# The MLP's second product by Strassen's scheme: seven block products for every two chunks and two token tiles

## The chip, the cores and the metric

The kernel runs on one core of one Trainium2 chip. The metric is the device time of one execution in microseconds (us); three runs of the kernel before took 801.2, 802.67 and 804.05 us, so its median is 802.67 us. The engines are named as in the profile: PE is TensorE (PEld its weight loads), DVE is VectorE, ACT is ScalarE, POOL is GpSimd, and SP is SyncE, whose queue issues most of the DMAs.

## What is computed

One transformer block on 2048 tokens of width 640. Its first half is an adaptive layer norm and a linear attention with 32 heads; its second half, which the change touches, is a second adaptive layer norm and an MLP with 1728 hidden features and a squared ReLU:

```python
h = _layernorm(x, axis=-1) * (1 + cb) + sb
x = x + gb * _B_ref(h, B_w1, B_b1, B_w2, B_b2)

def _B_ref(x, w1, b1, w2, b2):
    h = jnp.einsum("bsd,df->bsf", x, w1) + b1
    zero = jnp.zeros_like(h)
    r = jnp.where(h > zero, h, zero)
    h = r * r
    out = jnp.einsum("bsf,fd->bsd", h, w2) + b2
    return out
```

`sb`, `cb` and `gb` are vectors of 640 numbers worked out from the condition `c` and `w_mod`.

## The kernel before

All inputs are float32. Each operand of a large product is split into a high part, rounded to the type that TensorE reads in one pass (`fp32r`), and a low part, the rest; a product is then three matmuls, high by high, high by low and low by high (`three`, `mm` at line 76). ACT makes the high part with a copy, DVE the low part with a subtraction (`lo`, line 86). Every matmul of the kernel's products is put down to line 76 and every low part to line 86, so groups are told apart by their tiles.

The program has three stages: the projections with the attention's running sums; the attention's output with the product by `wo` (tile `pwo`); and the MLP. The MLP works on eight blocks (`j` = 0 to 7) of two token tiles, 256 tokens each, and on 14 chunks of hidden features (`f` = 0 to 13), 128 in each but the last, which has 64.

For each block and chunk `up(j, f)` makes the hidden values of 128 features for 256 tokens: 15 matmuls, five chunks of the width by three terms, with 256 columns moving (10 for the last chunk). They go to a bank of the pool `psB`, tile `up`. ACT applies the bias and the ReLU (line 1123), DVE squares (line 1124), ACT makes the high part (line 1125), and DVE the low part (line 86, tile `r`). Two chunks later `down(j, f)` takes the result as the stationary operand and the chunk of the second weight matrix, `W2[f]`, as the moving one: for each of the two token tiles, and for the columns 0 to 383 and 384 to 639 of the output (`CUT`), three matmuls into a bank of its own (`pj`, tiles `acc`), 12 in all (8 for the last chunk, where two terms are enough). The four banks collect over the 14 chunks. At the block's end DVE multiplies each by the gate (line 1155) and adds the residual (line 1156), and SP stores it (line 1160).

Beside that, a block makes the next block's input: loads (lines 965, 966), the sum with the attention's output (line 970) and its store (line 971), the layer norm (`ln_parts`: sums and squares on ACT, small steps on POOL at lines 318 to 325), ten transposes on PE (tile `tb`) whose results ACT scales (lines 347, 348) and DVE splits (`t_out`). During block 0, and a little before it, the two weight matrices are loaded (lines 901, 904), split on ACT (line 911) and DVE (line 86, tile `w`), and from then on they stay in SBUF.

The order of the work: in the stage ahead of the MLP the order of PE, DVE, ACT and POOL is written out by hand (`tc.manual_schedule`). In the MLP the instructions are given in the order of the loop, and a planner, which has its own costs, chooses the order on each engine. SP's order is the planner's in both. The only DMA that POOL issues stands at line 470, in the first stage.

Of the kernel before, what the change touches and what calls it, by code (L numbers as in the profile page):

```python
# [15 lines left out]
P = 128  # L16
# [21 lines left out]
W2_AT = 48  # L38
W_AT = (
# [5 lines left out]
W_LONG = {"w0", "w1", "w3", "w5", "w7", "w9", "w14", "w20", "k", "q0", "q1", "late0", "late1"}  # L45
BUFS = {"x": 2, "k": 2, "q0": 1, "q1": 1, "s1": 5, "s2": 2, "s3": 3, "s4": 5}
# [3 lines left out]
def kernel(  # L50
# [47 lines left out]
    tiny.tile([P, 16], F32, name="fill2")  # L98
    psA = ctx.enter_context(tc.tile_pool(name="psA", bufs=1, space=PS))
# [3 lines left out]
    def tok2(tag, name, at=0, pool=None):  # L103

        bufs = 1
        if tag == "w":
            tag = f"w{next(w_at)}"
        elif pool is None:
            bufs = BUFS[tag]
        t = (pool or mem).tile([P, 2 * D + (128 if tag in W_LONG else 0)], F32, tag=tag, name=name, bufs=bufs)  # L110
        return t[:, at : at + 2 * D].rearrange("p (s d) -> p s d", s=2)

    def row(tag, name):
        return mem.tile([P, D], F32, tag=tag, name=name, bufs=BUFS[tag])

# [43 lines left out]
    p12 = ExitStack()  # L159
    pc = p12.enter_context(tc.tile_pool(name="pc", bufs=1))  # L160
# [3 lines left out]
    mask5 = pc.tile([80, 40], F32, name="mask5")  # L164
    for v in vt:
        nc.gpsimd.memset(v, 0.0)
        nc.gpsimd.memset(v[:, :, 60:61], 1.0)
# [38 lines left out]
    def load_x(j):  # L206
        XB[j] = tok2("x", f"xb{j}")
# [103 lines left out]
    def ln_parts(xt, nm):  # L311
# [3 lines left out]
        for i in range(2):  # L315
            same = xt[:, i] if nm[0] == "a" else row("s3", f"same{nm}_{i}")
# [3 lines left out]
        for i in range(2):  # L320
            junk = row("s3", f"junk{nm}_{i}")
# [9 lines left out]
    def layer_norm(xt, nm):  # L331
        for _ in ln_parts(xt, nm):
# [12 lines left out]
    def t_out(cols, hT, d, nm, p):  # L345
        hf = row("s3", f"hf{nm}_{d}")[:, :256]
# [366 lines left out]
    psB = ctx.enter_context(tc.tile_pool(name="psB", bufs=3, space=PS, reuse_waits="tile"))  # L713
# [53 lines left out]
    def load_e(t):  # L767
# [4 lines left out]
        ET[t] = tok2(("k", "k", "x")[t % 3], f"el{t}")  # L772
# [112 lines left out]
    def prep_load(k, f, w):  # L885
# [6 lines left out]
        if EARLY_ROWS <= i < EARLY_ROWS + 4:  # L892
            if i % 2 == EARLY_ROWS % 2:
                RAWT.append(tok2("w", f"rawt{i}"))
# [29 lines left out]
    preps = [("1", f) for f in range(EARLY)]  # L924
    for f in range(NF):
        preps += [("2", f)] + ([("1", EARLY + f)] if EARLY + f < NF - 1 else [])
    preps += [("1", NF - 1)]
# [4 lines left out]
    def p_load(n=1):  # L932
        for _ in range(n):
            if todo["load"]:
                k, f = todo["load"].pop(0)
                prep_load(k, f, places.pop(0)(f"w{k}_{f}"))
# [19 lines left out]
    def load_x1(j):  # L956
        XM[j] = tok2("x", f"xm{j}")
        if j:
            XX[j] = [row("s2", f"xx{j}_{i}") for i in range(2)]
        else:  # L960
            both = tok2("x", "xx0")
# [6 lines left out]
    def add_x(j):  # L968
        for i in range(2):
            nc.vector.tensor_tensor(XM[j][:, i], XM[j][:, i], XX[j][i], op=ALU.add)  # L970
        nc.sync.dma_start(X1[j], XM[j])

    def layer2(j):
        add_x(j)
        layer_norm(XM[j], f"b{j}")

    def t2(j, d):
        if d == 0:
            H2[j] = ht(f"h2_{j}", j, (0, 96))
        t_unit(XM[j], cols_b, H2[j], d, f"b{j}", bank(f"tb{j}_{d}") if j == 0 or d % 2 else None)  # L980

    NB = NT // 2
    places += [new("w")] * 21 + [new(tag) for tag in ("k", "k", "q0", "q1")]
    places += [lambda nm, i=i: wslot(nm, f"late{i}", late[0]) for i in range(2)]
    places += [lambda nm: row("s1", nm)[:, None, :].bitcast(F32R)]
    assert len(places) == 2 * NF
# [30 lines left out]
    for j in range(NB):  # L1017
# [69 lines left out]
        if j == 5:  # L1087
            add_x(0)
# [11 lines left out]
        if j == 7:  # L1100
            p_hi(3)
            p_lo(4)
# [5 lines left out]
    late.append(ctx.enter_context(tc.tile_pool(name="late", bufs=1, reuse_waits="tile")))  # L1108

    def up(j, f):  # L1110
        p = bank(f"up{j}_{f}")
        terms = []
        n = FS[f]
# [5 lines left out]
        mm(p[:, :256], terms)  # L1119
        r = feat("s3", f"r{j}_{f}")  # L1120
        t = R2[j, f] = feat("s4", f"r2_{j}_{f}").bitcast(F32R)
        if n == P:
            nc.scalar.activation(r[:, 0], p[:, :256], AF.Relu, bias=b1_t[:, f : f + 1])  # L1123
# [137 lines left out]
```

## Time and profile before

| | us |
|---|---|
| median of three runs | 802.67 (801.2 to 804.05) |
| the profiled execution, its own time | 802.27 |
| its span, first to last instruction | 800.5 |
| first matmul of the MLP | 409.82 into the span |
| mean granted TensorE clock | 0.998 of full speed |

Times in the text are microseconds from the start of the span unless they are durations. A busy PE means that a matmul is somewhere in the pipe: the mean duration of one matmul in a group is about twice to two and a half times the distance between two of them, so the cost of a matmul is read from the chain of waits, where a run of 15 has its own length. Three views are used: the page's parts, the groups of instructions by line and shape, and the chain of waits that ended last, as a list in order of time.

### The profile page before, as it was taken

How to read it: one execution, taken by the hardware profiler on the slowest of the kernel's cores; microseconds unless marked ns; L12 is line 12 of the kernel's file. 1: busy time of each engine (PE TensorE's matmuls, PEld its weight loads, DVE VectorE, ACT ScalarE, POOL GpSimd, SP SyncE). 2: the span in 40 equal slices, each digit the busy share in tenths (PEclk: the TensorE clock that was granted, in tenths of full speed). 3: DMA queues.
4: the chain of work that ended last, by engine and by line, in shares of the span. 5: the costliest groups of instructions: out<-in, count | busy, mean ns of one | idle time of the engine just before them, and what ended most of it. 6: DMA issues, size and time to landing. Idle time of an engine off the chain costs nothing.

```text
span 800.5 us, 14885 instructions
## 1 busy us (share of the span) xinstructions
PE 789.8 (99%) x6085; PEld 761.6 (95%) x6085; DVE 494.8 (62%) x822; ACT 416.6 (52%) x942; POOL 75.0 (9%) x157
## 2 busy tenths in 40 slices
PE   9999999999999999999999999999999999999997
PEld 8899999999999878898899999999999999999997
DVE  4499889999788688993555753434434343353423
ACT  4667675576753355565777544354443534444321
POOL 3001021010000114331100000000000001000000
PEclk9999999999999999999999999999999999999999
DMA  8713326423120243321447330211303113030000
GB/s 325 293 35 128 114 83 203 147 85 115 67 100 1 80 168 132 116 83 67 148 142 253 117 132 2 97 68 34 133 2 130 34 67 100 1 132 1 35 1 34
DMA packets 30108, 80.13 MB, mean 100 GB/s; under 512 B 3600, under 2 KB 4112, under 8 KB 30040
## 3 DMA queue, kind: packets, MB, share of 16 engines
q1 hardware_dynamic: 27672, 73.83, 26.6%
q10 hardware_dynamic: 2304, 5.24, 1.7%
q8 instruction: 48, 0.79, 0.4%
q14 instruction: 20, 0.16, 0.1%
q0 software_dynamic: 64, 0.10, 0.0%
HBM read 55.47 MB, written 23.59 MB: 99 GB/s over the span
## 4 chain that ended last, share of the span: by engine, by line
PE 82%; DVE 8%; ACT 4%; DMA 2%; POOL 2%; issue 1%; SPq 0%; ACTq 0%; DVEq 0%; POOLq 0%
PE acc L76 23%; PE up L76 22%; PE pk L76 8%; PE pq L76 7%; PE pv L76 7%; PE pwo L76 5%; PE kvp L417 2%; DVE dn L785 2%; DVE scr L783 2%; PE te L824 2%; PE tb L337 1%; PE ta L337 1%; DMA xx<-in_x 1%; DVE ezb L804 1%; DMA raw_k<-in_wk 1%
## 5 line engine op out<-in xcount | busy, mean ns | idle before, releaser
L76 PE MATMUL acc<-w,r 128*128 128x256 f32 (+1 forms) x1312 | 216.0, 309 | 0.6 <-ACT r L1125 0.4
L76 PE MATMUL up<-h,w 128*128 128x256 f32 x1640 | 210.2, 276 | 0.0
L76 PEld LDWEIGHTS up<-h,w 128*128 128x128 f32 x1640 | 198.5, 188 | 0.1
L76 PEld LDWEIGHTS acc<-w,r 128*128 128x128 f32 x1312 | 196.9, 188 | 1.0 <-ACT r L1125 0.6
L1123 ACT ACTIVATE r<-up,b_t 128x256 f32<-128x256 f32 x104 | 48.8, 472 | 133.9 <-PE up L76 133.9
L1124 DVE TENSOR_TENSOR r<-r 128x256 f32<-128x256 f32 x104 | 43.8, 424 | 119.2 <-ACT r L1123 119.2
L76 PE MATMUL pwo<-wo,ot 128*128 128x256 f32 (+3 forms) x512 | 83.2, 315 | 0.1
L76 PE MATMUL pk<-wk,hT 128*128 128x384 f32 (+1 forms) x480 | 77.3, 312 | 0.9 <-ACT hT L348 0.9
L76 PEld LDWEIGHTS pwo<-wo,ot 128*128 128x128 f32 (+1 forms) x512 | 75.7, 188 | 1.9 <-ACT ot L861 0.4
L76 PE MATMUL pq<-wq,hT 128*128 128x384 f32 (+1 forms) x480 | 75.0, 311 | 0.4 <-ACT k L393 0.4
L76 PE MATMUL pv<-wv,hT 128*128 128x384 f32 (+1 forms) x480 | 75.2, 309 | 0.0
L76 PEld LDWEIGHTS pk<-wk,hT 128*128 128x128 f32 x480 | 71.7, 188 | 2.7 <-ACT hT L348 1.1
L1125 ACT ACTIVATE r<-r 128x256 fp32r<-128x256 f32 x104 | 42.8, 413 | 56.9 <-DVE r L1124 56.8
L76 PEld LDWEIGHTS pq<-wq,hT 128*128 128x128 f32 x480 | 70.7, 188 | 1.5 <-ACT k L393 0.9
L76 PEld LDWEIGHTS pv<-wv,hT 128*128 128x128 f32 x480 | 70.6, 188 | 0.4
L86 DVE TENSOR_TENSOR r<-r,r 128x256 fp32r<-128x256 f32 x112 | 47.2, 422 | 30.5 <-ACT r L1125 29.5
L86 DVE TENSOR_TENSOR h<-hfb,h 128x256 fp32r<-128x256 f32 x40 | 16.9, 424 | 28.9 <-ACT h L348 28.7
L445 DVE TENSOR_REDUCE rs_q<-eq 128x64 f32<-128x1280 f32 x16 | 23.5, 1472 | 14.8 <-ACT eq L404 14.8
L318 POOL TENSOR_SCALAR smb<-smb 128x2 f32<-128x2 f32 x8 | 1.8, 221 | 301.1 <-ACT sameb L317 301.1
L393 ACT ACTIVATE k<-pk 128x384 f32<-128x384 f32 (+1 forms) x32 | 13.0, 434 | 25.0 <-PE pk L76 24.9
L787 POOL TENSOR_TENSOR dn<-dn,rs_q 128x64 f32<-128x64 f32 x16 | 14.0, 873 | 128.1 <-DVE dn L785 128.1
L408 DVE TENSOR_REDUCE sk<-ek 128x64 f32<-128x1280 f32 x16 | 23.7, 1479 | 3.5 <-ACT ek L404 3.5
(185 smaller groups left out, 1039.9 us busy)
## 6 DMA issues: line engine op xcount, KB each, us to landing
esp<-eq SPq DMA_DIRECT2D x12, 640.0 KB, 3.1
el<-esp SPq DMA_DIRECT2D x12, 640.0 KB, 3.8
rw<-in_w SPq DMA_DIRECT2D x23, 320.0 KB, 3.4
wm<-in_w_mod SPq DMA_DIRECT2D x20, 320.0 KB, 3.8
xb<-in_x SPq DMA_DIRECT2D x8, 640.0 KB, 4.0
a<-at ACTq DMA_DIRECT2D x16, 320.0 KB, 2.1
xm<-a SPq DMA_DIRECT2D x16, 320.0 KB, 3.2
xx<-in_x SPq DMA_DIRECT2D x16, 320.0 KB, 3.3
```

What stands on the lines that cost most here:

```text
L76: nc.tensor.matmul(o, a, b, start=first and i == 0, stop=last and i == len(terms) - 1, skip_group_check=skip,)
L86: (eng or nc.vector).tensor_tensor(out_lo, full, hi.bitcast(F32), op=ALU.subtract)
L337: nc.tensor.transpose(p[:, i * P : (i + 1) * P], xn[:, i, d * P : (d + 1) * P], ident)
L408: nc.vector.tensor_reduce(s, heads(flat(e)), axis=AX.X, op=ALU.add)
L417: nc.tensor.matmul(kvp[64 * c : 64 * c + 64, g // 4, a : a + 2 * n].rearrange("p (s n) -> p s n", s=2), v[:, u], e[:, :, o : o + n], start ...
L445: nc.vector.tensor_reduce(s, heads(flat(e)), axis=AX.X, op=ALU.add)
L783: nc.vector.tensor_tensor(z, flat(ET[t]), flat(zb), op=ALU.mult)
L785: nc.vector.tensor_reduce(dn.rearrange("p s h -> p (s h)"), heads(z), axis=AX.X, op=ALU.add)
L824: nc.tensor.transpose(p[:m, a : a + P], EU[2 * j + i][:, b : b + m], ident)
L1123: nc.scalar.activation(r[:, 0], p[:, :256], AF.Relu, bias=b1_t[:, f : f + 1])
L1124: nc.vector.tensor_tensor(r[:, 1], r[:, 0], r[:, 0], op=ALU.mult)
L1125: nc.scalar.activation(t[:, 0], r[:, 1], AF.Copy)
```

## The change

Two chunks and two token tiles make a 2 by 2 matrix of 128 x 128 blocks, A11 and A12 for the first token tile, A21 and A22 for the second; the two chunks of the second weight matrix by the column ranges L (0 to 383) and R (384 to 639) make another, with ranges that are not equally wide. Before, the product of the two took eight block products. Now seven are formed, in the manner of Strassen: sums of the four A blocks (S1 to S4) are multiplied by weight chunks or sums of them. Four of the seven have a moving operand of 384 columns, three of 256. The seven results are collected over the pairs of chunks and combined once at the block's end.

- This form is used in blocks 2 to 7 for the pairs n = 0 to 5 (in block 7 for n = 0 to 4). The last pair, with the chunk of 64, the pair n = 5 of block 7, and the blocks 0 and 1 (`PLAIN = 2`) keep the eight products, as `down_plain`.
- The sums of the A blocks are made on DVE in every pair, from the squared values in float32; four blocks of sums are then split into high and low part (`split_s`) besides A11, A12, A22 (`split_a`).
- The sums of weights are made once, in block 1 and the start of block 2 (`t_load`, `t_sums`, `t_split`), and stored in DRAM (`TD`), three pieces for each pair: a and c of 128 x 2 x 384, b of 128 x 2 x 256 float32. One more sum takes the place of the range R of `W2[2n]` in SBUF. In blocks 2 to 7 every pair fetches its three pieces into small ring buffers with DMAs that POOL issues (`t_fetch`): two buffers for a, one for b, one for c.
- The accumulators: products 1, 2, 4 and 5 have one bank each, 3 shares a bank with the fourth plain region (`x`), 6 and 7 share one. The hidden values get one bank (`up`), its halves for even and odd chunks.
- The whole MLP's order on PE, DVE, ACT and POOL is now written by hand. Within a pair PE runs `up(j, 2n)`, the first part of the previous pair's products, `up(j, 2n+1)`, the second part. POOL takes over the sum of residual and bias (`add_bias`).
- The layer norm of the next block is cut into six pieces placed by hand (`LN_AT`...), transposes are done two units at a time, the weights of the MLP are split four at a time after every pair of block 0, and in the last step before the MLP `p_hi(3)` goes and `p_lo(4)` becomes `p_lo(3)`.

The core of the diff:

```diff
     def up(j, f):
-        p = bank(f"up{j}_{f}")
+        n, k = FS[f], f % 2
+        p = UP2[:, :256] if k and j < PLAIN else UP[:, 256 * k : 256 * k + 256]
...
+        t = FT[j, f // 2]
+        r = t[:, A12 : A22 + 1] if k else t[:, 0:8:7]
...
         if n == P:
-            nc.scalar.activation(r[:, 0], p[:, :256], AF.Relu, bias=b1_t[:, f : f + 1])
-            nc.vector.tensor_tensor(r[:, 1], r[:, 0], r[:, 0], op=ALU.mult)
-            nc.scalar.activation(t[:, 0], r[:, 1], AF.Copy)
-            lo(t[:, 1], r[:, 1], t[:, 0])
+            nc.scalar.activation(r, p, AF.Relu, bias=b1_t[:, f : f + 1])
+            nc.vector.tensor_tensor(r, r, r, op=ALU.mult)
+    def sums(j, n):
+        t = FT[j, n]
+        for o, a, b, op in ((S1, A21, A22, ALU.add), (S3, A11, A21, ALU.subtract),
+                            (S2, S1, A11, ALU.subtract), (S4, A12, S2, ALU.subtract)):
+            nc.vector.tensor_tensor(t[:, o], t[:, a], t[:, b], op=op)
+    def split_a(j, n, parts=(0, 1)):
...
+        if n < NP - 1:
+            nc.scalar.activation(a[:, 0, :3], t[:, :3], AF.Copy)
+            lo(a[:, 1, :3], t[:, :3], a[:, 0, :3])
+    def split_s(j, n):
+        t = FT[j, n]
+        a = RS[j, n] = p3.tile([P, 2, 4, P], F32, tag="rs", name=f"rs{j}_{n}").bitcast(F32R)
+        nc.scalar.activation(a[:, 0], t[:, S1 : S4 + 1], AF.Copy)
+        lo(a[:, 1], t[:, S1 : S4 + 1], a[:, 0])
+    RINGS = (("a", 384, 2), ("b", 256, 1), ("c", 384, 1))
+    def t_fetch(j, n, r):
+        RING[j, n, r] = ring(r, f"ring{j}_{n}_{r}")
+        nc.gpsimd.dma_start(RING[j, n, r], TD[n][r].bitcast(F32R))
+    def down_pair(j, n, part):
+        v, w = W2[2 * n], W2[2 * n + 1]
+        last = n == NF // 2 - 2 - (j == NB - 1)
+        if part:
+            todo = ("5", S1, RING[j, n, "a"], L), ("6", S2, v, R), ("3", S4, w, R), ("7", S3, RING[j, n, "b"], slice(0, 256))
+        else:
+            todo = ("1", A11, v, L), ("2", A12, w, L), ("4", A22, RING[j, n, "c"], L)
+        for reg, st, m, c in todo:
+            prod(j, reg, block(j, n, st), m, c, last and reg in "1567")
+    def first_combos(j):
+        y0, y1 = Y[j] = [row("s2", f"y{j}_{i}") for i in range(2)]
...
+        nc.scalar.activation(y0[:, L], p["1"], AF.Copy)
+        nc.scalar.activation(y1[:, 256:384], p["5"][:, 256:], AF.Copy)
+        add(y1[:, q], y0[:, q], p["6"])
+        add(y0[:, R], y1[:, q], p["5"][:, q])
+        add(y1[:, q], y1[:, q], p["7"])
+        add(y1[:, R], y1[:, q], p["5"][:, q])
+    def t_split(n):
+        a, b = TR_[n]
+        for r, w in (("a", a[:, L]), ("b", TR_[n, "b"][:, 1].bitcast(F32)), ("c", b[:, L]), (None, b[:, R])):
...
+            nc.scalar.activation(t[:, 0], w, AF.Copy)
+            lo(t[:, 1], w, t[:, 0])
+            if r:
+                nc.sync.dma_start(TD[n][r], t.bitcast(F32))
-    LAG = 2
-    seq = [(j, f) for j in range(NB) for f in range(NF)]
-    for n, (j, f) in enumerate(seq):
...
+    by_hand = tc.manual_schedule(engines={ET_.PE, ET_.DVE, ET_.Activation, ET_.Pool})
+    by_hand.__enter__()
+    for j in range(NB):
+        for n in range(NP):
...
+            up(j, 2 * n)
+            if prev and not plain(*prev):
+                split_s(*prev)
+            down(0)
+            if j < PLAIN:
+                layer(j + 1, 2 * n)
+            if 0 < m < NP - 2:
+                t_split(m - 1)
...
+            if twice:
+                t_fetch(j, n, "c")
+                t_fetch(j, n, "a")
...
+            up(j, 2 * n + 1)
...
+            split_a(j, n, (0, 1) if (j, n) != (NB - 1, NP - 1) else (1,))
+            if twice:
+                sums(j, n)
+            if j < PLAIN or n:
+                down(1)
+            if twice:
+                t_fetch(j, n, "b")
...
+            layer(j + 1, 2 * n + 1)
+            if 0 <= m < NP - 2:
+                t_sums(m)
...
+            prev = j, n
+    last_downs(NB - 1)
```

`down(k)` runs `down_plain` or `down_pair` for the previous pair, `twice` is true where the pair goes by the seven products, and `m` counts the pairs from the second of block 1 on. `add_bias(j)` adds the bias to the two residual tiles of a block on POOL, two additions of 128 x 640.

More of the change, by code (lines that the diff above doesn't have):

```diff
@@ L329, in ln_parts, with layer_norm @@
         yield
[L331 to L332 removed]
+    def layer_norm(xt, nm, spare=None):
+        for _ in ln_parts(xt, nm, spare):
             pass
```

389 lines of the change are left out of this document (291 added, 98 removed).

## The prediction

> **What bounds the kernel now.** I read the page first: the busy shares, and the chain that ended last.
>
> ```profile
> PE 789.8 (99%) x6085; PEld 761.6 (95%) x6085; DVE 494.8 (62%) x822; ACT 416.6 (52%) x942; POOL 75.0 (9%) x157
> ...
> PE 82%; DVE 8%; ACT 4%; DMA 2%; POOL 2%; issue 1%; SPq 0%; ACTq 0%; DVEq 0%; POOLq 0%
> ...
> L76 PE MATMUL acc<-w,r 128*128 128x256 f32 (+1 forms) x1312 | 216.0, 309 | 0.6 <-ACT r L1125 0.4
> L76 PE MATMUL up<-h,w 128*128 128x256 f32 x1640 | 210.2, 276 | 0.0
> ```
>
> PE is busy nearly always and carries 82% of the chain; its matmuls on `acc` and `up` waited 0.6 us in all. An average over stages proves little, so the busy times by block of the MLP come next (busy PE, PEld, DVE, ACT, POOL; then clock, DMA share, GB/s).
>
> ```profile
> 409.80:463.00 53.20, 52.56 (x414) 52.09 (x413) 37.01 (x71) 35.84 (x75) 1.31 (x4) 1.00 0.53 174
> ...
> 607.30:655.40 48.10, 48.10 (x382) 48.10 (x381) 19.88 (x48) 20.90 (x48) 1.59 (x4) 1.00 0.21 69
> ```
>
> In a later block PE never pauses, DVE and ACT are free more than half the time, the clock is full. There the end is set by how many columns PE streams. The chain of waits in order of time (start, length, what) gives the price of a matmul.
>
> ```profile
> 462.89 2.15 PE up L76 x19
> ...
> 607.21 2.15 PE up L76 x19
> 612.33 1.72 PE acc L76 x12
> ...
> 631.15 1.70 PE up L76 x15
> ...
> 655.31 2.15 PE up L76 x19
> ```
>
> 15 matmuls of 256 columns take 1.70 us: 0.113 each. The 12 of a chunk's `acc` are six of 384 and six of 256: 1.72 - 6 x 0.113 = 1.04, so 0.173 for one of 384. Width is what is paid for. The same mark returns after 655.31 - 607.21 = 48.10 us: one block.
>
> **The change part by part.**
>
> *What PE loses.* Two chunks cost 24 matmuls before, 12 of each width: 3.44 us. Seven products by three terms are 21: four products of 384 and three of 256, so 12 of 384 and 9 of 256, 3.10 us. Because the column ranges are unequal, the saved product is a narrow one: 3 x 0.113 = 0.34 us for a pair. Pairs: six in each of blocks 2 to 6, five in block 7, 35 in all. **Gain 35 x 0.34 = 11.9 us.** `up`, the transposes and the plain pairs keep their matmuls. Nothing else on PE's stream is late behind this gain so long as the other engines deliver; so the rest of the sum is stalls.
>
> *The steady pair, from its first `up`.* PE: `up` 0 to 1.70; products 1, 2, 4 (nine of 384, 1.56) to 3.26; second `up` to 4.96; products 5, 6, 3, 7 (1.54) to 6.50. The other engines' steps, with the hops between them, stand in the groups and in the time line of block 3's end:
>
> ```profile
> 603.88 0.47 ACT L1123 ACTIVATE r<-up,b_t 128x256 f32<-128x256 f32 x1 [3.08 <-PE up L76]
> ...
> 604.39 0.42 DVE L1124 TENSOR_TENSOR r<-r 128x256 f32<-128x256 f32 x1 [2.98 <-ACT r L1123]
> 604.85 0.42 ACT L1125 ACTIVATE r<-r 128x256 fp32r<-128x256 f32 x1 [0.49 <-DVE r L1124]
> ...
> 605.90 1.31 PE L76 MATMUL acc<-w,r 128*128 128x384 f32 x8
> 606.16 0.47 ACT L1123 ACTIVATE r<-up,b_t 128x256 f32<-128x256 f32 x1 [0.89 <-PE up L76]
> ```
> ```profile
> L86 DVE TENSOR_TENSOR r<-r,r 128x256 fp32r<-128x256 f32 x104 | 43.9, 422 | 29.8 <-ACT r L1125 29.5
> L347 ACT ACTIVATE hfb<-tb,cols_b 128x256 f32<-128x256 f32 x40 | 22.4, 560 | 0.8 <-ACT at L879 0.4 <-PE pwo L76 0.2
> L911 ACT ACTIVATE w<-rw 128x640 fp32r<-128x640 f32 x24 | 17.0, 730 | 5.8 <-DMA rw<-in_w 5.0 <-ACT at L879 0.8
> L970 DVE TENSOR_TENSOR xm<-xm,xx 128x640 f32<-128x640 f32 x16 | 13.1, 824 | 14.8 <-DMA xx<-in_x 14.8
> L1155 DVE TENSOR_TENSOR y<-acc,gb_b 128x384 f32<-128x384 f32 x16 | 8.9, 553 | 6.5 <-PE acc L76 6.5
> ```
>
> A hop from ACT to DVE or back is 0.04 us (603.88 + 0.47 to 604.39); ACT's ReLU starts 0.26 after PE has gone on to its next group (605.90 to 606.16). Between 256 columns (422 ns) and 640 (824) DVE pays 1.03 ns a column, so estimates are 0.29 us for 128, 0.55 for 384 (the row says 553), 0.69 for 512; ACT between 413 and 730 the same way: 0.52 for 384, 0.62 for 512.
>
> A blocks: the second ReLU starts at 5.22 and ends 5.69, square to 6.15, copy of three blocks to 6.7, low part to 7.3. Product 1 needs it at 6.50 + 1.70 = 8.20: **0.9 us in hand**. Sums: four times 0.29, to 8.45, which is 1.95 of the next pair; `split_s` copies after the first ReLU (2.43) to 3.05, low part to 3.8; product 5 needs it at 4.96: 1.2 in hand. DVE's work in a pair is 0.42 + 0.69 + 0.42 + 0.55 + 1.17 = 3.25 of 6.50 us, and a block's other DVE work (low parts of the transposes 5 x 0.42, sum with x 2 x 0.82, combining and four ends 3.6, gate and residual 4 x 0.82) adds 10.6 over seven pairs. DVE goes from 19.9 us to about 32 of 46 in a block, ACT from 20.9 to about 24. Both fit, and a misplaced piece of 0.8 us is what the margin takes. I take nothing for the steady pair here; if the cover went, a slip of 0.1 in every pair would be 3.5 us.
>
> *Block edges.* In the first pair of a block the second part of the products is only product x (5 x 0.113 = 0.57), so the A blocks have 1 us less, and DVE reads the accumulators of the last block in the same time (combining 4 x 0.42, three ends 1.5). The low part is ready at about 8.0 to 8.2 where PE arrives at 7.97. **0.2 us for each of six edges: 1.2** (between 0 and 1).
>
> *Blocks 0 to 2.*
>
> ```profile
> 595.82 0.22 PE tb L337 x2
> ...
> 606.06 1.15 PE acc L76 x8
> ```
> ```profile
> 409.82 9.20 PE L76 MATMUL up<-h,w 128*128 128x256 f32 x77
> ```
>
> Block 0: from 409.82, the first `up`, to the mark of block 1 less its 6.27 us (`up`, `acc`, `up`, `acc` x8: 1.70 + 1.72 + 1.70 + 1.15) is 46.8 us, where its matmuls take 45.0 (14 x `up`, 12 x `acc`, ten transposes at 0.11), so before lost 1.8 us on weights and loads. Three high parts more now lie in block 0 (3 x 0.73 of ACT); ACT, busy 35.84 us of that window's 53.20, hides them, without cover they cost 2.2. The first `down` waits for a weight and for the A blocks, about 1 us. I let new and old loss cancel (between -1.8 and +2.2). Block 1 gets the weight sums: for each pair three DVE operations of 256 (1.27), four ACT copies (1.86) and four low parts (1.94). With squares (0.85), splits (0.84) and a share of the next block's input (0.85) DVE's sum is 5.8 of a plain pair's 6.84. Where `t_split` stands behind two transposed units on ACT (2 x 0.98), the ReLU is some 2 us late and PE about 1.2; block 2 has one such place: **1.2 + 0.5**. SP gets 12 loads and 18 stores in these blocks, on which PE depends from block 2 on only; with its queue nearly idle I cost them at nothing.
>
> *The ring.* Every fetch waits on POOL until PE has left the buffer. Behind the fetch of c on POOL's queue stand that of a, the layer norm's small steps, for which ACT waits, and that of b, whose own wait is for the next part of the products. Buffer c is free at 3.26 and needed by product 4 of the next pair at 6.50 + 1.70 + 1.04 = 9.24: 5.98 us, less the hop 0.26: **5.7 us from issue to landing**; a has two buffers, b 5.9. One piece is 384 KB.
>
> ```profile
> el<-esp SPq DMA_DIRECT2D x12, 640.0 KB, 3.8
> ...
> xm<-a SPq DMA_DIRECT2D x16, 320.0 KB, 3.2
> ...
> wo<-wo POOLq DMA_DIRECT2D x1, 100.0 KB, 5.9
> ```
> ```profile
> 119.50 0.77 POOL L470 DMA_DIRECT2D wo<-wo  x1 [15.24 <-DVE wo L86]
> ```
> ```profile
> 119.50:123.00 3.50, 3.50 (x26) 3.50 (x25) 3.50 (x5) 2.11 (x6) 0.77 (x1) 1.00 0.72 231
> 123.00:125.50 2.50, 2.50 (x29) 2.16 (x29) 2.50 (x4) 0.63 (x1) 0.00 (x0) 1.00 0.98 336
> ```
>
> From below: a piece by SP's rows, 3.2 + 64 KB x 0.6 / 320 KB = 3.3 us. From above: POOL's only row, 5.9 for 100 KB, and 284 KB more at that rate, 0.5: 6.4. The first leaves 2.4 us in hand, the second is 0.7 late in each of the 29 pairs whose buffer was in use just before (five in blocks 2 to 6, four in block 7): 20 us. POOL's row is the nearest in kind; but while it ran (119.50 to 125.4) the DMA engines were busy by 0.72 and then 0.98, where a block of the MLP has 0.21 and the fetches (1.0 MB in 6.5 us) add about 0.4. So I take 5 us and late fetches only where the next block's loads meet them: **1.0** (between 0 and 20).
>
> The Trainium skill, "DMA: Bandwidth & Descriptors", section "Anatomy of one DMA — SWDGE (gpsimd) path", gives such a DMA 2.0 us and the bytes at 436 GB/s: 2.9 us for a piece. By it the ring costs nothing; POOL's row (5.9, where the rule says 2.2) disagrees; whether the load explains that, no row shows.
>
> *The tail.*
>
> ```profile
> 790.28 3.80 PE acc L76 x26
> ...
> 797.05 0.34 DVE y L1156
> ```
> ```profile
> out<-y SPq DMA_DIRECT2D x2, 192.0 KB, 1.8
> ...
> out<-y SPq DMA_DIRECT2D x2, 128.0 KB, 1.7
> ```
>
> The last product is now 384 wide: gate and sum 0.55 each for 0.42, and the last store has 192 KB for 128 (0.1 more): **0.4**. POOL adds for two regions earlier and runs beside.
>
> *The sum.* -11.9 + 1.2 + 1.2 + 0.5 + 1.0 + 0.4 = -7.6. The profiled execution took 802.27, which gives 794.7; the median shown is 0.4 above it: **795.1 us**.
>
> **The rivals.**
>
> *All of it hidden* (the edges, block 1 and the ring cost nothing): 802.7 - 11.9 + 0.4 = 791.2. For it speaks that PE waited 0.6 us in all before; against it the edge, where the sum of rows leaves no time.
>
> *The ring is late* (slower): each fetch of c takes 6.4 us as POOL's row scaled. It decides from 5.7 us on; at 6.4 it costs 29 x 0.7 = 20 us: 795 - 1 + 20 = 814. For it: the one row of that queue. Against: the load under which it was taken.
>
> *POOL's additions hold DVE.*
>
> ```profile
> L787 POOL TENSOR_TENSOR dn<-dn,rs_q x16: 318/869/1498, 273.2 to 384.9; 128x64 f32<-128x64 f32 x16
> ...
> L789 POOL TENSOR_TENSOR dd<-dn x16: 250/252/253, 274.7 to 385.3; 128x32 f32<-128x32 f32 x16
> ...
> L804 DVE TENSOR_TENSOR ezb<-el,dn x12: 1397/1401/1447, 276.6 to 347.9; 128x1200 f32<-128x1200 f32 x12
> ```
>
> The same POOL operation takes 318 to 1498 ns, as if it waited out a DVE operation of 1.4; DVE's spread is 50 ns, but these POOL pieces are short. From 252 ns for 32 columns and 318 for 64, one of 640 is about 1.5 us, and `add_bias` has two in a block. Where DVE has to wait for each, with 0.85 in hand, PE loses 7 x 2 x 0.65 = 9 us: 795 + 9 = 804, not told from no change. The Trainium skill, "SBUF — State Buffer", section "SBUF: two separate sides", makes it a lock: DVE with two SBUF inputs and POOL reading SBUF exclude each other for the whole instruction, whoever starts first. By it DVE waits too; the rows show only POOL waiting.
>
> **How the numbers follow.** A measurement of this kernel tells 0.3% (2.4 us) from no change, so faster is below 800.3. Forecast (792.5 to 798.5) 0.60; all hidden 0.14; POOL's additions 0.11, most of it within 0.3%; late ring 0.15, nearly all of it slower. That is faster 0.75, same 0.10, slower 0.15. The range reaches from the hidden case, a little below for block 0, to 790.0, and up past the additions to 806.0; the late ring beyond is left out.
>
> **What would show it.** Right: 105 matmuls of 256 columns are gone from the products; the mark of a block returns after 46.1 to 46.6 us, 2.0 less the edge; PE still busy in all of a block; DVE near 32 us. Wrong: PE waiting on a DMA in front of product 4, the fetch's time to landing above 5.7 us; POOL's additions beside long DVE operations and PE waiting on DVE's low parts; a block at 47 or more.

## The result, and the profile after

| | kernel before | changed kernel |
|---|---|---|
| median, lowest to highest | 802.45 us (801.20 to 804.05) | 829.63 us (825.40 to 830.64) |
| ratio, 95% interval | | 1.0328 [1.0294, 1.0363] |
| the profiled execution, its span | 802.27, 800.5 us | 825.4, 823.7 us |
| PE matmuls | 6085 | 5980 |

The changed kernel is 3.3% slower where 0.9% faster was forecast, and lies outside the range. (The profiled execution is the quickest of the changed kernel's, 4.2 us below the median, so its trace shows somewhat less than the median loss.) The page of the changed kernel: busy times, the chain that ended last, groups, and the ring's transfers.

```profile
PE 791.2 (96%) x5980; PEld 755.1 (92%) x5980; DVE 594.4 (72%) x1017; ACT 443.1 (54%) x987; POOL 165.7 (20%) x294
...
PE 30%; DVE 6%; ACT 2%; DMA 1%; issue 0%; POOL 0%; ACTq 0%; DVEq 0%; POOLq 0%
...
L77 PE MATMUL up<-h,w 128*128 128x256 f32 x1640 | 212.8, 282 | 16.1 <-DVE ft L1153 11.0
...
L87 DVE TENSOR_TENSOR h<-hfb,h 128x256 fp32r<-128x256 f32 x40 | 32.5, 813 | 49.7 <-ACT h L351 49.6
...
ring_c<-td_c POOLq DMA_DIRECT2D x35, 384.0 KB, 3.4
...
ring_a<-td_a POOLq DMA_DIRECT2D x35, 384.0 KB, 4.7
```

The 105 matmuls are gone. But `up`, which had waited 0.0 us, now waits 16.1, 11.0 of them for DVE's line 1153, a step of the narrow last chunk. And one kind of DVE operation has doubled: `h`, the low part of a transposed piece. The same group of the kernel before:

```profile
L86 DVE TENSOR_TENSOR h<-hfb,h 128x256 fp32r<-128x256 f32 x40 | 16.9, 424 | 28.9 <-ACT h L348 28.7
```

The mean rose from 424 to 813 ns with the same shape and count. A mean over 40 hides what it is made of, so the time line of one block's end comes next (start, length, engine, line; in brackets the idle time before and what ended it).

```profile
612.77 3.47 DVE L87 TENSOR_TENSOR h<-hfb,h 128x256 fp32r<-128x256 f32 x1 [1.08 <-ACT h L351]
612.87 3.07 POOL L1304 TENSOR_TENSOR xr<-xr,bb 128x640 f32<-128x640 f32 x2
...
616.16 0.41 DVE L1153 TENSOR_TENSOR ft<-up,ft 64x256 f32<-64x256 f32 x1
616.60 0.42 DVE L1154 SCALAR_TENSOR_TENSOR ft<-ft 64x256 f32<-64x256 f32 x1
616.62 1.99 PE L77 MATMUL up<-h,w 128*128 128x256 f32 x15 [2.24 <-DVE ft L1153]
```

An operation of 0.42 us took 3.47: about as long as POOL's two additions of the bias (3.07 together), which began 0.10 us after it, and its own time. What stands behind it on DVE comes 3 us late, and PE waits 2.24. In the code the bias belongs to the next block's first pair. POOL, however, had nothing left to wait for and ran ahead, so the additions fell into the last pair, where the chain transposes, `h`, next `up` has the least time in hand. The chain of waits has the same 3.47 at 661.93, 712.49 and 763.11, and 3.23 at 564.01: the ends of blocks 2 to 6.

The steady pair is what was forecast, and the block is not (chain of waits of the changed kernel; `acc` x9 returns each pair, `h` each block):

```profile
582.82 1.55 PE acc L77 x9
...
589.32 1.55 PE acc L77 x9
...
661.93 3.47 DVE h L87
...
712.49 3.47 DVE h L87
```

A pair is 589.32 - 582.82 = 6.50 us. A block is 50.56 where 46.1 to 46.6 was forecast and 48.10 was measured before.

The second new loss stands in block 2, once (two time lines):

```profile
529.75 4.29 DVE L1163 TENSOR_TENSOR ft<-ft 128x128 f32<-128x128 f32 x4
...
530.25 3.10 POOL L1304 TENSOR_TENSOR xr<-xr,bb 128x640 f32<-128x640 f32 x2
...
536.11 2.56 SPq L970 DMA_DIRECT2D xx<-in_x  x2
...
542.18 0.82 DVE L974 TENSOR_TENSOR xm<-xm,xx 128x640 f32<-128x640 f32 x1 [1.71 <-DMA xx<-in_x]
...
543.09 0.74 ACT L1381 ACTIVATE xx<-xm 128x640 f32<-128x640 f32 x1 [4.88 <-DVE xm L974]
...
546.34 3.57 PE L77 MATMUL up<-h,w 128*128 128x256 f32 x15 [4.97 <-ACT ft L1148]
```

It begins with the additions of the bias for block 1: four sums of A blocks take 4.29 us (1.01 at 528.37 in e1_no_bias below, without the additions), and what DVE does next, the last low parts of the weight sums, is late. Block 3's input is issued at 536 behind the stores of these sums. DVE waits for it, ACT waits 4.88 us for DVE with the ReLU of the running chunk queued behind, and PE waits 4.97 for the ReLU. The additions make this pause come later, they don't make it: e1_no_bias has one of 5.51 us at 544.08. The 15 matmuls after that pause take 3.57 us in place of 1.70. The windows (PE, PEld, DVE, ACT, POOL busy; granted clock, DMA share, GB/s) show the clock:

```profile
502.00:546.30 44.30, 36.35 (x271) 34.77 (x270) 30.72 (x67) 17.03 (x42) 11.04 (x17) 0.97 0.80 256
546.30:567.60 21.30, 19.23 (x134) 18.74 (x134) 12.17 (x24) 13.19 (x28) 9.09 (x14) 0.91 0.71 223
```

To see where the time went, I add up over the trace what each spacing between the starts of two matmuls has above 0.113 us (256 columns) or 0.173 (384). It counts waits and matmuls at a lower clock alike. A block counts from its first `up` to the next block's:

| us lost, by stretch | block 0 | block 1 | block 2 | blocks 3 to 6 | block 7 | sum |
|---|---|---|---|---|---|---|
| kernel before | 1.7 | 0.3 | 0.3 | 1.1 | 0.0 | 3.4 |
| changed kernel | 3.7 | 3.1 | 12.5 | 16.2 | 3.6 | 39.1 |

39.1 - 3.4 - 11.9 (the gain) = 23.8 us; the spans differ by 823.7 - 800.5 = 23.2. So the gain came as forecast, and three times as much was lost again, most of it in blocks 2 to 6.

### The profile page after: what moved, and what is told of

It reads as the page before. It is cut to its first block, busy times and chain, and to the rows that moved or that the text cites. A ratio compares the mean times of both kernels' runs of the same rounds, so it can differ in the third digit from the quotient of the medians.

```text
span 823.7 us, 15324 instructions
## 1 busy us (share of the span) xinstructions
PE 791.2 (96%) x5980; PEld 755.1 (92%) x5980; DVE 594.4 (72%) x1017; ACT 443.1 (54%) x987; POOL 165.7 (20%) x294
## 2 busy tenths in 40 slices
DMA packets 51104, 127.22 MB, mean 154 GB/s; under 512 B 5904, under 2 KB 7056, under 8 KB 51032
## 5 line engine op out<-in xcount | busy, mean ns | idle before, releaser
L77 PE MATMUL up<-h,w 128*128 128x256 f32 x1640 | 212.8, 282 | 16.1 <-DVE ft L1153 11.0
L1148 ACT ACTIVATE ft<-up,b_t 128x256 f32<-128x256 f32 x104 | 48.7, 468 | 111.2 <-PE up L77 110.7
L77 PE MATMUL acc<-w,ra 128*128 128x384 f32 x446 | 98.3, 341 | 2.0 <-ACT ra L1172 1.5
L1149 DVE TENSOR_TENSOR ft<-ft 128x256 f32<-128x256 f32 x104 | 45.7, 439 | 54.4 <-ACT ft L1148 53.4
L77 PEld LDWEIGHTS acc<-w,ra 128*128 128x128 f32 x446 | 73.4, 191 | 4.6 <-ACT ra L1172 1.9
L87 DVE TENSOR_TENSOR ra<-ft,ra 128x384 fp32r<-128x384 f32 (+2 forms) x85 | 37.7, 463 | 30.1 <-ACT ra L1172 18.6
L1256 POOL DMA_DIRECT2D ring_c<-td_c x35 | 19.0, 542 | 137.4 <-PE acc L77 114.5
L1163 DVE TENSOR_TENSOR ft<-ft 128x128 f32<-128x128 f32 x140 | 42.1, 341 | 1.2
L77 PE MATMUL acc3x<-w,ra 128*128 128x256 f32 x236 | 39.8, 281 | 1.6 <-DVE ra L87 1.6
L1172 ACT ACTIVATE ra<-ft 128x384 fp32r<-128x384 f32 x48 | 25.2, 525 | 29.7 <-DVE ft L1149 29.7
L77 PEld LDWEIGHTS acc3x<-w,ra 128*128 128x128 f32 x236 | 37.0, 190 | 2.0 <-DVE ra L87 1.8
```

What stands on the lines that cost most here:

```text
L77: nc.tensor.matmul(o, a, b, start=first and i == 0, stop=last and i == len(terms) - 1, skip_group_check=skip,)
L87: (eng or nc.vector).tensor_tensor(out_lo, full, hi.bitcast(F32), op=ALU.subtract)
L1148: nc.scalar.activation(r, p, AF.Relu, bias=b1_t[:, f : f + 1])
L1149: nc.vector.tensor_tensor(r, r, r, op=ALU.mult)
L1163: nc.vector.tensor_tensor(t[:, o], t[:, a], t[:, b], op=op)
L1172: nc.scalar.activation(a[:, 0, :3], t[:, :3], AF.Copy)
```

## The experiments

Four questions: what holds DVE; what stops PE in block 2; what the ring costs; and why a clean version still misses the forecast. Ratios are to the kernel before on the same chip, whose median was 801.59 us beside e1 to e4, and 801.96 to 802.2 beside the others. Where runs of two chips are compared, each is taken as its distance from that median.

| run | edit | us, median | ratio, 95% interval |
|---|---|---|---|
| e1_no_bias | no addition of the bias | 807.94 | 1.0082 [1.0067, 1.0097] |
| e2_bias_dve | the addition on DVE | 810.68 | 1.0110 [1.0094, 1.0125] |
| e3_memset | POOL only writes in its place | 804.18 | 1.0039 [1.0024, 1.0054] |
| e4_pieces | POOL adds 128 columns at a time | 810.39 | 1.0127 [1.0084, 1.0169] |
| h1_before_pool_add | kernel before, its addition on POOL | 804.33 | 1.0035 [1.0021, 1.0048] |
| f1_late_ln3 | e2, block 3's input later | 807.90 | 1.0070 [1.0054, 1.0085] |
| f2_all | f1, three smaller repairs | 804.91 | 1.0039 [1.0025, 1.0053] |
| g1_sp_by_hand | f2, SyncE in the written order | 806.99 | 1.0053 [1.0039, 1.0067] |
| p3_three_plain | f2, three plain blocks for two | 806.26 | 1.0057 [1.0043, 1.0071] |
| g2_no_ring | g1, no ring traffic from block 3 on | 804.75 | 1.0033 [1.0021, 1.0045] |
| g3_no_ring_at_all | f2, no ring traffic after its first pair | 800.27 | 0.9978 [0.9969, 0.9986] |
| k1_ring_on_sp | f2, the ring fetched by SyncE | 801.85 | 0.9999 [0.9990, 1.0007] |
| o1_bias_early | k1, bias before the block's end | 802.93 | 1.0006 [0.9998, 1.0015] |
| o2_both | o1, block 3's input earlier again | 802.66 | 1.0009 [1.0000, 1.0018] |

### What holds DVE

**e1_no_bias**: the addition of the bias is left out.

```diff
     def add_bias(j):
-        for i in range(2):
-            nc.gpsimd.tensor_tensor(XR[j, i], XR[j, i], bb, op=ALU.add)
+        pass
```

> Leaves out the sum of residual and bias (add_bias), so the bias of the second product is missing from the output. Theory A (POOL's two additions of 128 x 640, 3.1 us back to back, hold DVE's two-input operations, and PE waits for DVE): the PE gaps of 2.3 to 2.5 us before five block edges (about 12 us), those at 452 (1.0), 534 to 536 (2.0) and 804 (1.2), part of the 5.3 at 541 and most of the half-speed stretches of the clock behind them (about 5) go: 829.6 falls to 804 to 811. Theory B (DVE and ACT are simply too full for the order written by hand; DVE would be late without POOL too): at most 4 us less, 825 or more.

Measured 807.94, theory A: 6.4 us above the kernel before, where the changed kernel was 829.63 - 802.45 = 27.2 above. Sixteen additions cost 20.8 us. `h` is back at its old length:

```profile
L87 DVE TENSOR_TENSOR h<-hfb,h 128x256 fp32r<-128x256 f32 x40 | 17.4, 435 | 51.7 <-ACT h L351 51.6
```

**e2_bias_dve**: the same additions as `nc.vector.tensor_tensor`.

> The same additions, at the same place of the order, on DVE instead of POOL (0.82 us each instead of 1.55). Theory A: the long DVE operations of 3.5 to 4.3 us vanish, DVE has 1.64 us more at each block's first pair: 806 to 815, a little above the run that leaves them out. Theory B (DVE too full): DVE gets 11 us more work, so 830 or more.

810.68, theory A again: the same work on DVE, busy 71 to 72% of the span, costs 18.1 us less than on POOL with its 20%.

**e3_memset**: POOL is kept busy as long, but reads nothing (`scratch` is a tile of its own, 128 x 64; the bias is missing here too).

```diff
-        for i in range(2):
-            nc.gpsimd.tensor_tensor(XR[j, i], XR[j, i], bb, op=ALU.add)
+        for i in range(18):
+            nc.gpsimd.memset(scratch, 0.0)
```

> In place of the additions POOL sets a scratch tile of 128 x 64 to zero 18 times, about 3 us of POOL in the same place, which writes SBUF but reads nothing; the bias is missing from the output. If it is POOL's reading of SBUF that holds DVE: as the run that leaves the additions out, within 2 us (804 to 811). If what counts is that POOL is busy, so that its later fetches are issued late: as the changed kernel, 825 to 831.

804.18. The time line at the end of block 2:

```profile
556.94 3.75 POOL L1306 MEMSET scratch<- 128x64 f32 x18
557.11 0.43 DVE L87 TENSOR_TENSOR h<-hfb,h 128x256 fp32r<-128x256 f32 x1 [0.21 <-ACT h L351]
557.66 0.42 DVE L1153 TENSOR_TENSOR ft<-up,ft 64x256 f32<-64x256 f32 x1
```

POOL is busy for 3.75 us and `h`, in the same place, takes 0.43. So POOL's being busy doesn't hold DVE; what counts is that it reads SBUF while DVE has two inputs there. That is the rule of the Trainium skill, "SBUF — State Buffer", section "SBUF: two separate sides", that the prediction set beside its rival, and here DVE does wait.

The run is also 3.8 us faster than e1_no_bias, where 2 us either way was expected. Most of that lies in block 2, which loses 4.5 us here and 9.6 in e1 by the measure above: behind the memsets POOL issues two fetches at 533.23 and 533.75 (531.56 and 532.08 in e1), DVE has begun on both halves of block 3's input by 537.5 (541.92 in e1), and PE's wait of 5.51 us for the ReLU in e1 becomes one of 2.17 us for a ring piece. When POOL's fetches go out matters, then; that they alone delayed the input in e1 no run shows.

**e4_pieces**: five additions of 128 columns for each of 640.

> The same additions on POOL, each in five pieces of 128 columns, about 0.45 us each. If DVE waits for one POOL instruction at a time, it gets in between the pieces and its longest hold falls to 0.5 us: 805 to 814. If POOL keeps DVE out as long as its instructions follow each other, DVE is held for all ten, some 4 to 4.5 us: 832 to 842.

810.39, in the expected range. The time line shows that short pieces are no sure help all the same:

```profile
559.60 4.18 POOL L1305 TENSOR_TENSOR xr<-xr,bb 128x128 f32<-128x128 f32 x10
559.74 4.32 DVE L87 TENSOR_TENSOR h<-hfb,h 128x256 fp32r<-128x256 f32 x1 [0.21 <-ACT h L351]
```

One DVE operation waited out ten additions in a row. Elsewhere DVE got in between: of its operations beside such pieces only two more took over 1.0 us (1.08 and 1.07). What decides between the two no run shows.

**h1_before_pool_add**: in the kernel before, its addition of the bias (line 1140) moves to POOL, with nothing else changed.

> The kernel before, with its own sum of residual and bias (line 1140) on POOL instead of DVE: two additions of 128 x 640 in each block. The hold is the same in any kernel: DVE operations of 2 to 3.5 us should appear eight times. What it costs depends on the cover: there a chunk's result is used two chunks (6.8 us) later, and its chain takes about 2.6, so DVE may be some 3 to 4 us late. Expected 802 to 805 (less than 0.5 us for a block); if a hold always costs PE its own length, 8 x 2.4 = 19 us more, 821.

804.33: 2 us, not 20. The same addition, but here it mostly waits for its loads and falls where DVE is free, and the eight long DVE operations that were expected don't appear. Where it doesn't wait, DVE is held just so (time line):

```profile
445.38 7.37 POOL L1140 TENSOR_TENSOR xr<-xr,bb 128x640 f32<-128x640 f32 x4 [10.08 <-DMA xr<-x]
...
445.74 1.79 DVE L1124 TENSOR_TENSOR r<-r 128x256 f32<-128x256 f32 x1
447.45 1.79 DVE L86 TENSOR_TENSOR h<-hfb,h 128x256 fp32r<-128x256 f32 x1
```

Four additions, and DVE operations of 0.42 us that take 1.79 each; PE waits once, 1.99 us at 453.49. So the hold is nothing new in the changed kernel. New is that it meets the one pair with no time in hand, in each block.

### What stops PE in block 2

**f1_late_ln3** (on e2): sum, normalization and transposes of block 3's input stand one step later in the order by hand.

```diff
-    LN_AT2 = {"load": 5, "add": (7, 7), "ln": (7, 7, 8, 8, 9, 9), 10: (0, 1), 11: (2, 3), 12: (4,)}
+    LN_AT2 = {"load": 5, "add": (8, 8), "ln": (8, 8, 9, 9, 10, 10), 11: (0, 1), 12: (2, 3), 13: (4,)}
```

> The additions on DVE, and in block 2 the next block's sum, layer norm and transposes one half pair later (LN_AT2: sum at 8, transposes at 11 to 13). Theory: the second loss is a burst of transfers in pairs 2 to 4 of block 2 (weight sums out, x in, output out, residual in, beside the fetches), behind which the sum with x is late on DVE, and ACT and PE behind it; in the run with the additions on DVE it shows as PE gaps of 1.3, 3.5 and some half-speed clock at 538 to 547, 5 to 6 us in all. With 3 us more for the transfers it falls by 3 to 5: 810.7 goes to 805 to 808. Rival: PE waits there for the fetch of c as well, and the burst only moves the wait: 809 or more.

807.90, 3.3 less. The pause (3.19 us in e2, at 543.43) is gone; in its place PE waits for the ring (1.63 us at 543.47, 0.50 at 550.80) and, at the end of the block, some 2 us, in part for the last transposed piece, which is now late.

**f2_all** (on f1): block 2's residual is loaded one pair later (the lines below), one split of weight sums moves to a freer place, and POOL's last sum on `y` goes in pieces of 128 columns.

```diff
-            if n == (5, 6, 4)[min(j, 2)]:
+            if n == (5, 6, 5, 4)[min(j, 3)]:
                 residual(j)
```

> The run before this one, and besides: the residual loads of block 2 one pair later (out of the burst), the fourth split of weight sums in block 1 behind the A blocks instead of ahead of the ReLU (a PE gap of 1.6 at 502), and POOL's last two additions of 128 x 640 in pieces of 128 columns (a PE gap of 2.0 near the end, where DVE is held). Each gap should go for the most part: 801 to 804, level with the kernel before. If the gaps only move, 805 to 808.

804.91, just above the expectation. What is left in block 2 is the wait for a ring piece (time line), with the DMA engines busy throughout (windows; the last three columns are clock, DMA share, GB/s):

```profile
541.43 0.62 PE L77 MATMUL acc<-ring_b,rs 128*128 128x256 f32 x3 [2.09 <-DMA ring_b<-td_b]
```
```profile
535.00:540.00 5.00, 4.07 (x30) 3.70 (x28) 2.63 (x5) 2.46 (x6) 1.29 (x3) 1.00 1.06 379
540.00:545.00 5.00, 3.56 (x26) 3.57 (x27) 2.42 (x8) 3.14 (x7) 1.68 (x4) 1.00 1.09 400
```

**g1_sp_by_hand** (on f2): SyncE's loads and stores keep the written order too, so that the residual comes later; in f2 the planner still issues it right behind the stores. The residual of blocks 3 to 6 is also written one pair later, a line that the diff here leaves out.

```diff
-    by_hand = tc.manual_schedule(engines={ET_.PE, ET_.DVE, ET_.Activation, ET_.Pool})
+    by_hand = tc.manual_schedule(engines={ET_.PE, ET_.DVE, ET_.Activation, ET_.Pool, ET_.SP})
```

> The kernel with all repairs (f2_all, span 802.8) still had PE waiting about 6 us for ring pieces, most of it where the DMA engines were busy all the time (535 to 545, share 1.06). Here SP's loads and stores also keep the written order, so the residual loads come late and one block apart. Theory A (what is left is a burst that SP's early loads make): ring waits fall to about 3 us, time 800 to 803, level with before or just below it. Theory B (a fetch on POOL's queue is late by its own latency, whatever else is moved): the waits stay, 804 to 806.

806.99: a miss, above both theories. The wait for the ring in block 2 remains (1.10 us at 541.82) and one for the ReLU (1.43 at 543.87) is back. To spread SyncE's transfers in this way was no help.

**p3_three_plain** (on f2): three blocks in the old scheme, the seven products from block 3 on.

```diff
-PLAIN = 2
+PLAIN = 3
```

> f2_all (804.9 us) with three plain blocks for two: the weight sums are made in block 2, the seven products begin in block 3, 29 pairs for 35, so 2.0 us of the gain go. Theory A (the stall of the first block with seven products belongs to the change-over itself: last weight sums, late residual, compressed input): it moves along to block 3, one block's ring waits and edge (1 to 1.5 us) are saved, time 804.5 to 807. Theory B (it belongs to what else block 2 does): it is gone, 798 to 801.

806.26, theory A: the loss moves along. PE now waits 1.52 us for `ring_b` at 589.75, in block 3. So it belongs to the first block of seven products, in which the last weight sums, the late loads and the ring come together, and not to what else block 2 does.

### What the ring costs

**g2_no_ring** (on g1) and **g3_no_ring_at_all** (on f2): one pair's pieces are read again (the diff is that of g3; g2 has block 3 for block 2).

```diff
     def t_fetch(j, n, r):
+        if (j, n) > (2, 0):
+            RING[j, n, r] = RING[2, 0, r]
+            return
```

> As g1_sp_by_hand, but from block 3 on the weight sums of that block's first pair are read again instead of being fetched for each pair (the second products of blocks 3 to 7 use wrong weights, so that part is left out of what is computed; the matmuls are the same). It prices the ring in these blocks. Theory A (late pieces cost PE what the gaps show, 3 to 4 us in blocks 3 to 7 of f2_all): 2 to 4 us below g1_sp_by_hand, 797 to 801, and a block of 46.1 to 46.6 us from mark to mark. Theory B (the gaps only show waits that something else would make anyway): within 1 us of g1_sp_by_hand, with the gaps then behind DVE or ACT.

> f2_all (804.9 us), but after the first pair of block 2 the weight sums of that pair are read again instead of being fetched for each pair (the second products of blocks 2 to 7 use wrong weights, so that part is left out of what is computed; the matmuls are the same). Theory A (the PE gaps of 530 to 568 in block 2 come from transfers: the ring's 1.0 MB a pair on top of the next block's input, the residual and the stores): they fall from 6.5 us to 2 or less, and 2 us more go in blocks 3 to 7, time 797 to 800. Theory B (the gaps of block 2 come from the order on ACT and DVE, where the input's layer norm stands ahead of the ReLU): they stay at 4 to 6, time 801 to 803.

g2 takes 2.2 us less than g1: theory A as to the difference, though not as to the time, since g1 was itself slower than expected; and a block returns after 46.88 us from block 4 on, still above the 46.1 to 46.6 expected. g3 takes 4.6 less than f2, 800.27, just above theory A's range. The wait at 541 is gone, but 554 to 559, where the late transposes are, still loses 1.8. So the ring costs f2 4.6 us, half of it in block 2. And with no ring at all the scheme is only 0.2% below the kernel before.

**k1_ring_on_sp** (on f2): the same pieces, fetched by another queue.

```diff
-        nc.gpsimd.dma_start(RING[j, n, r], TD[n][r].bitcast(F32R))
+        nc.sync.dma_start(RING[j, n, r].bitcast(F32), TD[n][r])
```

> f2_all (804.9 us), with the ring's fetches issued by SyncE's queue and not by POOL's; the same pieces from the same place. The prediction had its two bounds from these two queues: 3.3 us for a piece by SP's rows, 6.4 by POOL's. f2_all measured 3.9 (c), 4.5 (a), 3.5 (b) at the median on POOL's queue, and PE waited some 6 us for late pieces. Theory A (the queue sets the landing): medians of 3.0 to 3.5, ring waits half as long, 800.5 to 803. Theory B (landing is set by what the DMA engines have to move, and SyncE's own loads and stores now stand ahead of fetches): medians as before or longer, 804 to 808.

801.85, theory A, and level with the kernel before. The ring's transfers on the page of f2_all and on that of k1_ring_on_sp (the last number is the median from issue to landing):

```profile
ring_c<-td_c POOLq DMA_DIRECT2D x35, 384.0 KB, 3.9
...
ring_a<-td_a POOLq DMA_DIRECT2D x35, 384.0 KB, 4.5
...
ring_b<-td_b POOLq DMA_DIRECT2D x35, 256.0 KB, 3.5
```
```profile
ring_c<-td_c SPq DMA_DIRECT2D x35, 384.0 KB, 3.0
...
ring_a<-td_a SPq DMA_DIRECT2D x35, 384.0 KB, 3.6
...
ring_b<-td_b SPq DMA_DIRECT2D x35, 256.0 KB, 3.8
```

The large pieces land 0.9 us sooner, the small one 0.3 later (it stands behind two others). The edit also moves the pieces as float32 in place of fp32r; the packets and bytes of all queues together are the same (51104 and 127.22 MB), but no run parts the type from the queue. Of PE's waits for the ring over half a microsecond one is left, 1.36 us at 537.98 in block 2. The prediction's price by SyncE's rows, 3.3 us, lies between the two medians of 384 KB on SyncE's queue; issued by POOL, as in f2 and in the change, they take 0.9 more in f2.

### What is left

k1 loses 15.7 us by the measure of the table above (3.4, 1.5, 3.5, 5.8 and 1.4 in the stretches of that table), 12.3 more than before: the gain, and no more. The two largest parts were tried.

**o1_bias_early** (on k1): the bias is added in the last two pairs of a block, one tile each, and no longer in front of the square of the next block's first pair.

```diff
+            if 3 <= j < NB - 1 and n >= NP - 2:
+                add_bias(j, (n - NP + 2,))
```

> k1_ring_on_sp (801.85 us), with the bias of blocks 3 to 6 added on DVE one and two pairs before the block's end, one tile at a time behind the low part of the S blocks, and no more in the first pair of the next block, where the two additions (1.55 us) stand in front of the square. Theory A (the edges cost 0.8 us each because of those additions, not because of the sum of the steps alone): PE's stalls at the starts of blocks 4 to 7 fall to 0.2 to 0.4 each, 799.5 to 801. Theory B (the edge is short of time anyway, as the prediction's 8.0 to 8.2 against 7.97): the stalls stay, or a late low part comes before the edge in place of them, 801.5 to 803.

**o2_both** (on o1): of block 3's input the last two pieces of the layer norm and three of the five transposed units come one step earlier again.

```diff
-    LN_AT2 = {"load": 5, "add": (8, 8), "ln": (8, 8, 9, 9, 10, 10), 11: (0, 1), 12: (2, 3), 13: (4,)}
+    LN_AT2 = {"load": 5, "add": (8, 8), "ln": (8, 8, 9, 9, 9, 9), 10: (0,), 11: (1, 2), 12: (3, 4)}
```

> o1_bias_early, with the normalization and the transposes of block 3's input one step earlier (the one moved for f1_late_ln3 stood too late: PE waits some 2 us at 555 to 558 for the last transposed part). Theory A (those 2 us are that wait): 798 to 800, and faster than the kernel before by 0.25 to 0.5%. Theory B (earlier, ACT waits for the input again and ReLU stands behind it): the wait moves to 536 to 546, no gain, 800 to 803.

Both went theory B's way: 802.93 and 802.66, not to be told from k1. In o1 the low part in the first pair of a block is on time and a low part in the last pair is late instead: 1.1 us a block, as before. In o2 the wait for the last transposed piece becomes three others (time line of PE):

```profile
545.67 0.33 PE L339 MATMUL tb<-ident,xm 128*128 128x128 f32 x1 [0.48 <-ACT xm L1393]
546.49 0.33 PE L339 MATMUL tb<-ident,xm 128*128 128x128 f32 x1 [0.48 <-ACT xm L1393]
...
558.15 1.98 PE L77 MATMUL up<-h,w 128*128 128x256 f32 x15 [0.87 <-DVE ft L1153]
```

So what is left isn't one misplaced step. In these pairs a repair moves the wait to the next place; why there is no slack in all of them at once I haven't settled. No version that computes the whole beats the kernel before.

## Why the prediction was wrong

**The gain**, 11.9 us: right. 105 matmuls of 256 columns are gone and the steady pair is 6.50 us.

**The step that failed** is that the sum has no term for POOL's additions. They stand only as the rival "POOL's additions hold DVE", with a chance of 0.11 and the price: "Where DVE has to wait for each, with 0.85 in hand, PE loses 7 x 2 x 0.65 = 9 us". The mechanism was named there, and e1, e2 and e3 show it; it cost 20.8 us. Four things that the price left out stand in the trace; how much each adds was not tried alone. First, the two additions follow each other on POOL and DVE is held through both: 3.47 us as one, not twice 1.5 with 0.85 in hand each time, so 3.47 - 0.42 = 3.05 against one margin; PE waits 2.06 to 2.24 at the ends of five blocks. Second, I priced them where the code has them, in a first pair; POOL, which has no wait in front of them, had run ahead into the last pair. Third, one pair of additions stands at the start of block 2, ahead of the last weight sums, and PE waits there for another 1.7 us (0.43 at 534.76 and 1.27 at 536.64). Fourth, behind two of the five waits at block ends the granted clock was lower (below). The chance was off too: "the rows show only POOL waiting" was weighed as evidence against a hold of DVE, but those POOL pieces lasted 0.25 to 0.32 us where undisturbed, too short to show one, as the prediction itself noted. That left the rule of the Trainium skill with nothing against it.

**Block 2**, 0.5 us: wrong. Costed as one late `t_split`, it lost 12.5 in the changed kernel, and 3.5 even in k1. The transfers were costed at nothing "with its queue nearly idle"; but in that block the last sums' stores, the next input, the residual, the outputs and the ring meet (DMA share 1.06 and 1.09 above), and ACT's queue carries a late load on to PE.

**The ring**, 1.0 us between 0 and 20: the size was off. On POOL's queue it costs 4.6 (f2 against g3). The medians, 3.4 to 4.7 us in the changed kernel, lie between the two bounds and below the 5 that I took, but single pieces in block 2 need more than the 5.7 in hand. The Trainium skill's 2.9 us, "DMA: Bandwidth & Descriptors", section "Anatomy of one DMA — SWDGE (gpsimd) path", lies below every median of a 384 KB piece on that queue. That the queue matters, the one thing POOL's row of before had said, k1 bears out with 3.1 us, the type of the pieces aside.

**Block edges**, 0.2 each: too small. In k1 (time line of PE; the same two rows as at the start of each later block):

```profile
657.77 2.03 PE L77 MATMUL up<-h,w 128*128 128x256 f32 x15
659.72 1.57 PE L77 MATMUL acc<-w,ra 128*128 128x384 f32 x6
```
```profile
704.79 2.03 PE L77 MATMUL up<-h,w 128*128 128x256 f32 x15
706.76 1.57 PE L77 MATMUL acc<-w,ra 128*128 128x384 f32 x6
```

A block returns after 704.79 - 657.77 = 47.02 us, where 48.10 - 6 x 0.34 = 46.06 would be free of stalls: 0.96 lost a block. In that stretch the usual `up` x15 takes 1.87 and `acc` x6 1.20 (at 668.26 and 666.70), so 0.16 + 0.37 of it stand in these two rows: the second `up` waits for the ReLU of the first, and the A blocks' low part is late.

**Blocks 0 and 1**: in k1 block 0 lost 1.7 more than before, inside its bound of +2.2 but not cancelled, and block 1 1.3 more, near the forecast 1.2. In the changed kernel it was 2.0 and 2.8; block 1 has one wait of 1.32 us there, at 504.45, for a high part on ACT, and in f2, which moves a split, it is gone. The prediction counted only the three differences of weights that DVE makes for each pair; POOL makes two more, and they hold DVE as well: 1.11 us for an operation of 0.55 at 491.96. What that costs no run shows. **The tail**: POOL's two last sums "run beside" was wrong in the changed kernel (PE waits 1.55 us for a low part beside them at 816.11); in pieces they do.

Put together, with the additions off POOL, the input moved and the ring on SyncE, the terms are -11.9 + 1.7 + 1.3 + 3.2 + 4.7 + 1.4 = +0.4 (the gain, then what k1 loses more than the kernel before in blocks 0, 1, 2, 3 to 6, and 7) where -7.6 was forecast, and k1 measured level. The scheme's gain is real, but the work that it gives to DVE, ACT and the DMA engines takes it back.

## What to carry to other kernels

An addition moved to POOL isn't free because POOL is idle: look for what DVE runs beside it, and price the hold at worst by POOL's whole run of such operations, not by one; and ask where the queue really runs them, since an engine without waits runs ahead of the order on paper. Where a change saves a fraction of a microsecond in each of many steps, the budget of the other engines in the fullest step decides, not in the average one. A price that two queues give differently should be tried on the cheaper queue before it is hidden by order.

## What the hardware showed that I had not expected

- A DVE operation can be held through a whole run of POOL's reading operations: in seven of the changed kernel's eight pairs of additions one operation took 3.23 to 3.56 us, and 4.32 through ten pieces in e4. Elsewhere the two alternated (1.79 us each in h1). In the rows the held operation even begins before POOL's first (612.77 and 612.87), so the start in the trace doesn't decide it: the rule "whoever starts first", which the prediction has from the Trainium skill, "SBUF — State Buffer", section "SBUF: two separate sides", doesn't fit these two starts.
- POOL that only writes doesn't hold DVE: `h` took 0.43 us beside 18 memsets.
- A pause of PE can be followed by a lower granted clock: 0.97 and 0.91 in the windows up to and behind the wait of 4.97 us, where 15 matmuls took 3.57 us in place of 1.70. Behind waits of 2.24 us it went both ways (windows, as above; the clock is the third number from the right):

```profile
616.60:619.60 3.00, 2.98 (x23) 2.98 (x24) 1.69 (x6) 1.38 (x4) 0.00 (x0) 1.00 0.38 104
665.80:668.80 3.00, 3.00 (x16) 3.00 (x17) 1.20 (x4) 0.42 (x1) 0.00 (x0) 0.58 0.41 105
```

The chain has 1.99 us for the 15 matmuls at 616.62 and 3.19 at 665.78; 2.63 at 716.34 and 1.99 at 766.96 are the next two. So a wait can cost more than its length; what decides it these runs don't show.
